# A new issue order for a fused attention and gated feed-forward kernel on one core

## The chip, the core and the metric

The kernel runs on one core of a Trainium2 chip. Five engines with queues of their own work on it: TensorE (PE in the profile; PEld is its loading of weights), VectorE (DVE), ScalarE (ACT), GpSimd (POOL) and SyncE (SP), which here does nothing but issue all DMAs. Each engine works through its instructions in the order in which they were issued, and waits where an operand or a buffer is not there yet. The metric is device time in microseconds, the median of several runs.

## What is computed

```python
scores = scale * np.matmul(x, state.transpose(0, 1, 3, 2))      # B, H, S, D = 8, 8, 512, 64; 32 states
a = softmax(scores);   xread = np.matmul(a, state)
scores2 = scale * np.matmul(state, x.transpose(0, 1, 3, 2))
a2 = softmax(scores2); sread = np.matmul(a2, x)
attn = np.concatenate([xread, sread], axis=2)                   # 8 x 544 rows in all, 512 columns
h = attn @ w_in                                                 # 512 -> 1024
solu = h * softmax(h)
ln = (solu - mean) / np.sqrt(var + 1e-06) * g_ln
out = ln @ w_out                                                # 1024 -> 512
```

Everything is float32 in and out. (`softmax` stands for the reference's lines with maximum, exp and sum.)

## The kernel before

The rows of `attn` are cut into 34 tiles of 128 rows: tiles 0 to 31 are token reads, four for each of the eight batches b, and tiles 32 and 33 are the state reads. The attention's second product is folded into the weights: since `xread @ w_in` is `a @ (state @ w_in)`, the kernel forms state times w_in for each b once and multiplies the softmax with it.

Most products of fp32 data are made as three products of fp32r parts (high times high, high times low, low times high). An operand is split by a copy (the high part) and a difference (the low part). Batch 0's h products, tiles 0 and 1's output products, and everything on the small states are plain fp32 instead, and each such product has two entries in the profile.

The work is cut into named steps, written as Python generators; each name below is a token of the order. A token runs the step to its next `yield`.

- `l0`..`l7` load half row blocks of w_in (`l0 l2 l4 l6` are the left halves), `l8`..`l15` load w_out, `Ls` the states, `LT` and `Ln` the two layouts of x, `Lg` the gains. Each load but the gains is half a megabyte. `cl` and `c` turn a loaded weight (64-bit words) into fp32: one ScalarE step, two VectorE steps and an addition on VectorE or GpSimd.
- `G` copies the states on GpSimd. `V b n` multiplies the states of batch b with half n of w_in (eight small fp32 products, tiles swps or swph in PSUM) and copies the result out. For b of 2 and above it goes to DRAM and back (`Y`, `Z`) until `P` splits it (tiles swh, swl). For b of 0 and 1 it stays.
- `S b` makes the scores of a batch (eight small products), `A b` (`Ah` for batch 0) the softmax of the token reads (tile a, then ath and atl), `E b` that of the state reads with a bounce through DRAM (e2d, e2), and `R b` their reads (srps, srT, sreadT).
- `H t` makes h of tile t (ps_h, two PSUM tiles), `C t` the chain on it (maximum, exp, product, shift by the mean, square, four tiny GpSimd steps for the scale), `D t` transposes u in blocks and sends it through DRAM and back (ut, back), `T t` splits the transposed u (uh, ul), and `O t` multiplies with w_out, scales and stores (o, osb).
- `wi` splits w_in, which only the state reads' tiles need whole; `wg` scales w_out by the gains and `wo` splits it.
- `K` is a warm-up: a product of the identity with itself on TensorE, whose result nobody reads.

What sets the order around everything is the string ORDER: `issue` walks it and runs one step of the named generator at each token, with no scheduler behind it. Since each engine takes its instructions in that order, ORDER is five queues in one. The table OPT names, step by step, the engine of every copy, difference and similar operation (`a`, `d`, `p` for ScalarE, VectorE, GpSimd). Tiles of 4 KB a row come from one pool of 45 slots, so a load also waits for the last reader of its slot; PSUM has two tiles for h and four single banks.

## Time and profile before

| | |
|---|---|
| median of 3 runs | 379.31 us (378.69 to 380.57) |
| span of the profiled execution | 375.6 us; what lies around it is not in the profile, the median is 3.7 us above the span |
| TensorE clock granted, mean | 0.990 |
| DMA | 92.17 MB, mean 245 GB/s |
| idle of GpSimd's scale steps, waiting for ScalarE's square | 57.3 us |
| idle of ScalarE's exp, waiting for the maximum on VectorE | 40.8 us |

How to read the lines that follow below: the page's first line has each engine's busy time, share and instructions; its digit rows cut the span in 40 slices and give busy tenths. A row of the view of stretches has, for a start and an end, busy time and count by engine, the granted clock, the share of DMA time and GB/s. A row of the chain has start, duration, engine, tensor, line and count. A row of the timeline has start, duration, engine, line, operation, output and input with their shapes, the count, and in brackets how long the engine was idle before and what ended that. A row of the grouped view ends with total busy us, mean ns of one, and the idle time before.

### The profile page before, as it was taken

Reading aid. Unit: us, or ns where it says so; the run is one execution under the profiler, and the core shown is the slowest. Engines: PE = TensorE matmul, PEld = TensorE weight load, DVE = VectorE, ACT = ScalarE, POOL = GpSimd, SP = SyncE. Lnnn points to the kernel's source line nnn. Section 1 sums busy time; section 2 is a strip of 40 time slices with the busy share of each in tenths; the row PEclk is TensorE's granted clock in tenths of the full one; section 3 lists DMA queues with packets and bytes.
Section 4 is the critical chain, followed back from the end, with each engine's and each line's share of the span. In section 5 each row is a group of like instructions: output and inputs, shape, how many; then the busy total and the mean of one; then the engine's idle time right before and its main releaser. Section 6 shows DMA issues by size and latency. Waiting matters only on the chain.

```text
span 375.6 us, 6452 instructions
## 1 busy us (share of the span) xinstructions
PE 360.5 (96%) x2382; PEld 266.7 (71%) x2382; DVE 316.7 (84%) x436; ACT 202.5 (54%) x332; POOL 156.3 (42%) x220
## 2 busy tenths in 40 slices
...
PEclk9999999889999999999999999999999999999999
...
GB/s 250 408 393 389 209 314 415 407 292 246 184 264 193 283 298 273 259 306 278 270 316 182 271 272 383 199 119 126 298 169 173 203 134 225 61 294 94 140 168 58
DMA packets 47050, 92.17 MB, mean 245 GB/s; under 512 B 4140, under 2 KB 25900, under 8 KB 47020
## 3 DMA queue, kind: packets, MB, share of 16 engines
...
## 4 chain that ended last, share of the span: by engine, by line
PE 65%; DVE 17%; issue 6%; DMA 6%; ACT 3%; POOL 1%; SPq 0%; DVEq 0%; POOLq 0%
PE o L535 32%; PE h L461 20%; PE warm L559 6%; DMA back<-ut 5%; DVE u L474 3%; PE swps L188 2%; DVE ub L498 2%; DVE ul L136 2%; PE sps L188 2%; DVE sm L468 1%; DMA ut<-ub 1%; DVE a L383 1%; PE swph L188 1%; DVE z L378 1%; PE srps L410 1%
## 5 line engine op out<-in xcount | busy, mean ns | idle before, releaser
L535 PE MATMUL o<-wohi,ul 128*128 128x512 f32 (+1 forms) x264 | 71.5, 385 | 1.0 <-DVE ul L136 1.0
L535 PE MATMUL o<-wohi,uh 128*128 128x512 f32 (+1 forms) x264 | 70.9, 385 | 1.0 <-ACT uh L131 0.8
L535 PE MATMUL o<-wolo,uh 128*128 128x512 f32 (+1 forms) x264 | 70.9, 384 | 0.0
L136 POOL TENSOR_TENSOR ul<-back,uh 128x512 fp32r<-128x512 f32 x33 | 45.4, 1382 | 55.8 <-ACT uh L131 30.7
L471 ACT ACTIVATE e<-h,sm 128x1024 f32<-128x1024 f32 x34 | 37.8, 1113 | 40.8 <-DVE sm L468 40.8
L535 PEld LDWEIGHTS o<-wohi,uh 128*128 128x128 f32 x264 | 48.4, 188 | 12.4 <-ACT uh L131 1.2
L535 PEld LDWEIGHTS o<-wohi,ul 128*128 128x128 f32 x264 | 48.4, 188 | 11.1 <-DVE ul L136 1.4
L468 DVE TENSOR_REDUCE sm<-h 128x1 f32<-128x1024 f32 x34 | 41.3, 1214 | 17.1 <-ACT osb L542 12.4
L535 PEld LDWEIGHTS o<-wolo,uh 128*128 128x128 f32 x264 | 48.5, 188 | 9.8
L486 ACT ACTIVATE e<-u 128x1024 f32<-128x1024 f32 x34 | 36.0, 1058 | 31.9 <-DVE u L481 31.5
L474 DVE SCALAR_TENSOR_TENSOR u<-h,e 128x1024 f32<-128x1024 f32 x34 | 41.1, 1212 | 3.9 <-ACT e L471 3.9
L498 DVE STREAM_TRANSPOSE ub<-u 128x1024 f32<-128x1024 f32 x34 | 41.9, 1236 | 1.8 <-ACT u L479 1.2
L461 PE MATMUL h<-swh,ath 128*128 128x512 f32 x112 | 36.4, 409 | 2.8 <-DVE u L474 2.7
L542 ACT ACTIVATE osb<-o,sm 128x512 f32<-128x512 f32 (+1 forms) x25 | 16.6, 664 | 37.2 <-PE o L535 32.9
L461 PE MATMUL h<-swl,ath 128*128 128x512 f32 x112 | 35.9, 406 | 0.0
L461 PE MATMUL h<-swh,atl 128*128 128x512 f32 x112 | 35.4, 397 | 0.0
L490 POOL TENSOR_TENSOR sm<-sm 128x1 f32<-128x1 f32 x34 | 9.7, 285 | 57.8 <-ACT e L486 57.3
L461 PEld LDWEIGHTS h<-swh,ath 128*128 128x128 f32 x112 | 21.2, 194 | 10.5 <-issue 5.9
L131 ACT ACTIVATE uh<-back 128x512 fp32r<-128x512 f32 (+1 forms) x38 | 23.4, 623 | 8.3 <-DMA back<-ut 8.2
L479 ACT ACTIVATE u<-u,sm 128x1024 f32<-128x1024 f32 x17 | 19.5, 1149 | 13.5 <-DVE u L474 13.3
L559 PEld LDWEIGHTS warm<-ident 128*128 128x128 f32 x182 | 23.3, 211 | 4.8 <-issue 3.4
L461 PEld LDWEIGHTS h<-swl,ath 128*128 128x128 f32 x112 | 20.9, 193 | 7.2 <-issue 1.7
...
## 6 DMA issues: line engine op xcount, KB each, us to landing
ut<-ub SPq DMA_DIRECT2D x34, 512.0 KB, 3.5
back<-ut SPq DMA_DIRECT2D x34, 512.0 KB, 4.4
...
xT<-xT_dram SPq DMA_DIRECT2D x16, 512.0 KB, 7.2
xn<-xn_dram SPq DMA_DIRECT2D x16, 512.0 KB, 7.3
kept<-vt SPq DMA_DIRECT2D x12, 512.0 KB, 7.7
swf<-kept SPq DMA_DIRECT2D x12, 512.0 KB, 6.8
raw<-w_in_dram SPq DMA_DIRECT2D x8, 512.0 KB, 8.2
```

The lines of the kernel that those rows point to most:

```text
L131: nc.scalar.activation(out, src, AF.Copy)
L136: engine(k).tensor_tensor(out=out, in0=a, in1=hi.bitcast(F32), op=ALU.subtract)
L188: nc.tensor.matmul(banks[j][at:at + NS, :], state_of(b, head), moving(head // 2)[h * D:(h + 1) * D], start=True, stop=True)
L461: nc.tensor.matmul(ph[t][:, cols], left[l][:, p, tok], right[r][:, cols], start=(p, l, r) == (0, 0, 0), stop=(p, l, r) == (parts - 1, *kin ...
L468: nc.vector.tensor_reduce(nm, ph[t], AX.X, ALU.max, negate=True)
L471: nc.scalar.activation(e, ph[t], AF.Exp, bias=nm, accum_out=z)
L474: nc.vector.scalar_tensor_tensor(out=u, in0=ph[t], scalar=1.0, in1=e, op0=ALU.mult, op1=ALU.mult, accum_out=su)
L479: nc.scalar.activation(u, u, AF.Identity, bias=su, scale=-float(DF))
L486: nc.scalar.activation(e, u, AF.Square, scale=float(DF) ** -0.5, accum_out=ss)
L498: nc.vector.transpose(ub, us[t][0])
L535: nc.tensor.matmul(po, ut[t][l][:, f, :], w[NP + f // 2][:, f % 2, cols], start=(hf, l, w is wohi, q) == (0, 0, True, 0), stop=(hf, l, q) ...
L559: nc.tensor.matmul(warm, ident, ident, start=True, stop=True)
```

## The change

No step is rewritten. ORDER is a new string, and OPT names other engines for some operations. By the number of instructions: VectorE gives to GpSimd seven swl differences, eight weight conversions, three ul, two atl, a wlo and a wolo difference and four of the softmax's subtractions and products; VectorE gives four ath, two swh and nine uh copies to ScalarE and takes from it four copies out of V's banks, two w_in and one w_out split copies, two scalings and six shifts of u.

```diff
-OPT = dict(ph=2, k4=45, direct=[0, 1], hn=[0], vh=[0, 1], ah=[0], on=[0, 1], s2='pppp', add='dpdpdpdpddpddddp',
-           whi='aaaa', wlo='dddp', wg='aaaaaaaa', woh='aaaa', wol='dpdp', ev='aaaaaaaaaaaaaaaaaaaaaaaaaaaaaaaa',
-           swh='aaadaadaadaadddad', swl='pppppdpdpdddppdd', sub='dpddpddp', subh='dpdd', mulh='dpdd', mul='pddddpdd',
...
+OPT = dict(ph=2, k4=45, direct=[0, 1], hn=[0], vh=[0, 1], ah=[0], on=[0, 1], s2='pppp', add='ppdpppdppppppppp',
+           whi='dada', wlo='dppd', wg='aaddaaaa', woh='aaad', wol='ppdp', ev='aaaaaaaadaaadaaaadadaaaaaaaaaaaa',
+           swh='aaadaaddaaaaaadd', swl='pppppppppppppppp', sub='dpddppdp', subh='dpdddpdddpdddpdd',
...
 ORDER = """
-K l0 l2 Ls0 l4 Lg l6 l1 l3 c0 cl0 LT00 c0*2 cl2 LT01 c2*3 G0 Ls2 c4 cl4 l5 G0 c4 l7 cl6 l8 c4 c6 cl1 Lg c6*2 c1 cl3
-Ln00 K*60 V00 c3*2 V10 c1 Ln01 V00 c3 V00 V20 V10 Ln10 V10 c1 V20 l9 V20 K*5 V30 G2 wi0 c5 l10 G2 c5 V30 l11 V30
...
+l0 l4 c0*2 c4 cl0 c0 K l2 c4 c2 K*3 c2 l6 c6 K*5 cl4 c4 Ls0 cl2 l3 l5 c2 cl6 G0 c6*2 c5*2 G0 V30*2 LT00 LT01 c3*2 V00
+V30 V20*2 cl5 c5 K*2 cl3 K l7 cl7 l1 V00 c7 l9 Ls2 c7 S0 Ah00 c1 c3 Ah00 c1 K Ah00*2 c7 l8 Lg*3 K cl1 c1 V10 V20 E0 Lg
...
```

Three places show what the order does. The first is SyncE's queue at the start of the program, before (raw is a loaded weight block, st the states, gT the gains, xT a layout of x):

```order
L209 DMA raw_85<-w_in_dram 128x1024
L209 DMA raw_87<-w_in_dram 128x1024
L165 DMA st_89<-stB_dram 128x1024
L209 DMA raw_91<-w_in_dram 128x1024
L156 DMA gT<-g_dram 128x2x1
L209 DMA raw_94<-w_in_dram 128x1024
L209 DMA raw_96<-w_in_dram 128x1024
L209 DMA raw_98<-w_in_dram 128x1024
```

and the same queue after:

```order
L201 DMA raw_83<-w_in_dram 128x1024
L201 DMA raw_85<-w_in_dram 128x1024
L201 DMA raw_97<-w_in_dram 128x1024
L201 DMA raw_106<-w_in_dram 128x1024
L157 DMA st_118<-stB_dram 128x1024
L201 DMA raw_122<-w_in_dram 128x1024
L201 DMA raw_124<-w_in_dram 128x1024
L185 DMA xT_0_149<-xT_dram 128x1024
```

The four left halves of w_in now come first (before, the fourth was the sixth entry), the states behind them, and the gains move behind the second states' load.

The second place is TensorE's queue at its start, before (warm is the warm-up, swph and swps are V's results, wf the converted w_in, s the states):

```order
L559 MATMUL warm<-ident 128x128 x61
L188 MATMUL swph_0_209<-wf_100,s_0_116 32x512 x2
L188 MATMUL swph_0_209<-wf_112,s_0_116 32x512 x2
L188 MATMUL swph_0_209<-wf_120,s_0_116 32x512 x2
L188 MATMUL swph_0_209<-wf_135,s_0_116 32x512 x2
```

and after (the first V is that of batch 3, then batches 0 and 2, then S0):

```order
L551 MATMUL warm<-ident 128x128 x9
L180 MATMUL swps_0_0_138<-wf_87,s_0_129 32x512 x2
L180 MATMUL swps_0_0_138<-wf_100,s_0_129 32x512 x2
L180 MATMUL swps_1_0_139<-wf_90,s_0_129 32x512 x2
L180 MATMUL swps_1_0_139<-wf_108,s_0_129 32x512 x2
L180 MATMUL swph_0_157<-wf_87,s_0_129 32x512 x2
```

Sixty-one warm-ups became nine ahead of the first V. In the whole program 91 became 23.

The third place is TensorE's queue between the scores of block 1 and those of block 2, before (o is the output of a tile, h_802 and h_811 are tiles 4 and 5; the scores of block 2 follow):

```order
L529 MATMUL o_0_738<-wog_580,uh_729 128x512 x2
L529 MATMUL o_0_738<-wog_742,uh_729 128x512 x2
L529 MATMUL o_0_738<-wog_754,uh_729 128x512 x2
L529 MATMUL o_0_738<-wog_766,uh_729 128x512 x2
L461 MATMUL h_802<-swh_0_778,ath_796 128x512 x2
L461 MATMUL h_811<-swh_0_778,ath_796 128x512 x2
L461 MATMUL h_811<-swl_0_789,ath_796 128x512 x2
L461 MATMUL h_802<-swl_0_789,ath_796 128x512 x2
L461 MATMUL h_811<-swh_0_778,atl_805 128x512 x2
L461 MATMUL h_811<-swh_1_787,ath_796 128x512 x2
L461 MATMUL h_802<-swh_0_778,atl_805 128x512 x2
L461 MATMUL h_802<-swh_1_787,ath_796 128x512 x2
```

and after (o_0_655 is tile 0, o_0_672 tile 1, h_743 tile 4):

```order
L521 MATMUL o_0_655<-wog_617,uh_637 128x512 x2
L521 MATMUL o_0_672<-wog_554,uh_657 128x512
L521 MATMUL o_0_672<-wog_617,uh_657 128x512 x2
L521 MATMUL o_0_655<-wog_609,uh_637 128x512 x2
L521 MATMUL o_0_672<-wog_609,uh_657 128x512
L521 MATMUL o_0_655<-wog_698,uh_637 128x512 x2
L453 MATMUL h_743<-swh_0_420,ath_712 128x512 x2
L453 MATMUL h_743<-swl_0_572,ath_712 128x512 x2
L521 MATMUL o_0_672<-wog_609,uh_657 128x512
L180 MATMUL sps_0_756<-xT_0_695,s_0_129 32x512 x4
L180 MATMUL sps_1_757<-xT_1_619,s_0_129 32x512 x4
```

Before S2 there now stand 14 output products of tiles 0 and 1 in place of 8 of tile 0, and 4 h products in place of 16.

More of the change, by code (lines that the diff above doesn't have):

```diff
@@ L27 @@
 NTILES = B * NT + B * NS // P
-OPT = dict(ph=2, k4=45, direct=[0, 1], hn=[0], vh=[0, 1], ah=[0], on=[0, 1], s2='pppp', add='dpdpdpdpddpddddp',
-           whi='aaaa', wlo='dddp', wg='aaaaaaaa', woh='aaaa', wol='dpdp', ev='aaaaaaaaaaaaaaaaaaaaaaaaaaaaaaaa',
-           swh='aaadaadadaadddad', swl='pppppdpdpdddppdd', sub='dpddpddp', subh='dpdd', mulh='dpdd', mul='pddddpdd',
-           ath='aaddaddd', alo='dddpddpd', up='aaadaadaaaddddaaaaadddddaaddaddadd',
-           uh='aadaaaaaaaadaaddaaaaadaadaaadddddadddaaddddaaddadaaaaaaddddaddaadadd',
-           ul='ppppdpdpppdppdpddpdppddpddpddddppdddpdpddppppdppdddddpppppdpppddppdp',
-           oe='aaaaaaaddaaaaaaaaaadadddadaaaddada')
@@ L83 @@
-T30 H32*2 O28 T30 O28 T30 O28*3 O29 O28 O29*2 T31 C32 O28 O29*2 T31 O29 C32 O29*2 T31 C32 O29*3 T31 O29 C32 O30*2
-D32 C32 O31 O30 O29 O30 D32 C32 O30 C33 O29 O30*3 C33 O30 O31 D32 O30 C33 O30*2 C33 O31*2 D33 C33 O31*2 O30 O31 D33
-C33 O31 O30 T32 O31*2 T32 O31 O32 O31 T32 D33 O32 O31 T32 O32*2 O31 O32*6 T33 O32 T33 O32 T33 O33 O32 O33 T33 O33*3
-O32 O33*23
+OPT = dict(ph=2, k4=45, direct=[0, 1], hn=[0], vh=[0, 1], ah=[0], on=[0, 1], s2='pppp', add='ppdpppdppppppppp',
+           whi='dada', wlo='dppd', wg='aaddaaaa', woh='aaad', wol='ppdp', ev='aaaaaaaadaaadaaaadadaaaaaaaaaaaa',
+           swh='aaadaaddaaaaaadd', swl='pppppppppppppppp', sub='dpddppdp', subh='dpdddpdddpdddpdd',
+           mulh='ppdddpdddpdddpdd', mul='pdpdppdd', ath='aaaadaaa', alo='dppdddpp',
+           up='adddddadddddddddaaaaadddddaddaaadd',
+           uh='aaaddaadaaaaaaaadaaadaaadaaaddaaaaaaaaaaaaadddaddddaaadaddaaadadadaa',
+           ul='ppppppdpdpppppppdppdppdpdddddpdddpdddpdpppdppdppddpppddppdppppdddpdp',
+           oe='aadaaaaaadaaadaadddaadaaddaaaaddaa')
@@ new lines @@
+ORDER = """
+l0 l4 c0*2 c4 cl0 c0 K l2 c4 c2 K*3 c2 l6 c6 K*5 cl4 c4 Ls0 cl2 l3 l5 c2 cl6 G0 c6*2 c5*2 G0 V30*2 LT00 LT01 c3*2 V00
+V30 V20*2 cl5 c5 K*2 cl3 K l7 cl7 l1 V00 c7 l9 Ls2 c7 S0 Ah00 c1 c3 Ah00 c1 K Ah00*2 c7 l8 Lg*3 K cl1 c1 V10 V20 E0 Lg
+V10*2 Ah01 K*2 G2 Ah00 l10 Ah00 V00 K*2 E0 K*2 E0 K*3 Ln00 E0 G2 V11 Ah00 V11 E0*2 Ah01*2 V40 Ah00*2 V40 V11 V01 V40
+V01 V50 H0 V01 Lg l12 c8 c9 c8 c12 l11 Ah01 V50*2 cl8 l13 Ah01 l14 V21*2 H0 V21 cl10 c10 E0 c12 cl12 c12 P11 Ah01 l15
+V60*2 H1 c11 H1 C0*2 V60 Ah01 LT10 LT30 E0*2 P10 C0*2 LT11 V31 C0 V31 Ah01*2 H2 P11 C1 D0 V70 c9 V31 C1 Ln01 H2 c8 V70
```

78 lines of the change are left out of this document (35 added, 43 removed).

## Prediction

> **What bounds the kernel now.** I read the page's busy shares first, then its clock line, then a few stretches of time, then the chain that ended last.
>
> ```profile
> PE 360.5 (96%) x2382; PEld 266.7 (71%) x2382; DVE 316.7 (84%) x436; ACT 202.5 (54%) x332; POOL 156.3 (42%) x220
> PEclk9999999889999999999999999999999999999999
> ```
>
> ```profile
> core 0: us, PE busy (x) PEld busy (x) DVE busy (x) ACT busy (x) POOL busy (x), PEclk, DMA share, GB/s
> 70.00:80.00 10.00, 7.71 (x26) 4.83 (x34) 9.96 (x11) 7.66 (x13) 7.90 (x10) 0.66 0.96 372
> 80.00:290.00 210.00, 208.87 (x1350) 161.15 (x1335) 199.97 (x269) 114.79 (x188) 100.63 (x139) 1.00 0.71 243
> 290.00:310.00 20.00, 17.77 (x135) 13.52 (x133) 18.36 (x25) 9.54 (x15) 3.65 (x7) 1.00 0.52 178
> ```
>
> ```profile
> 1.34 16.39 PE warm L559 x122
> ...
> 20.47 1.31 PE warm L559 x10
> 21.78 1.02 PE swps L188 x16
> ...
> 24.11 1.02 PE sps L188 x16
> ...
> 32.63 1.91 PE h L461 x4
> ...
> 237.41 13.15 PE o L535 x58
> ...
> 324.43 0.94 PE h L461 x4
> ...
> 370.62 0.47 ACT osb L542
> ```
>
> TensorE is busy 96% of the span, and from 80 to 290 us it idles 1.1 us while VectorE is busy 200 of 210: two engines are full at once. The chain shows the pitch of TensorE's work: 227 ns for an fp32r product of 512 columns (13.15 / 58), 1.02 us for a group of eight small fp32 products (V or S), 131 ns for a warm-up entry. The profile has two entries for each fp32 product; the 182 warm-up entries are 91 products in the code, and 182 x 131 ns = 24 us of the 360 are no work. The change leaves 46 entries, 6 us; every other product stays. So 18 us of "busy" goes, but the span shortens only by what the next wait allows. I therefore count by stages with three marks: the first H product (32.6), the scores of block 1 (S1, 57.6) and of block 2 (S2, 79.7), and the last product (370.6).
>
> **Stage A, up to the first H: 4.0 us earlier.**
>
> ```profile
> 4.72 0.68 ACT L221 ACTIVATE r<-raw 128x512 uint32<-128x512 uint32 x1 [2.73 <-DMA raw<-w_in_dram]
> 5.98 0.68 ACT L221 ACTIVATE r<-raw 128x512 uint32<-128x512 uint32 x1 [0.57 <-DMA raw<-w_in_dram]
> 8.10 1.65 POOL L133 COPY s<-st 64x512 f32<-64x512 f32 x2 [6.81 <-DMA st<-stB_dram]
> 12.89 0.69 DVE L238 CUSTOM_DVE_ANT_0 wf<-wf,r 128x1024 uint16<-128x1024 uint16 x1
> 17.66 1.95 PE L188 MATMUL swph<-wf,s 64*32 64x512 f32 x32
> ```
>
> Before, the operands of the first V were complete at 12.89 + 0.69 = 13.6 us (the last conversion of a first-half w_in tile), but the 122 warm-up entries stood ahead of it in TensorE's order until 17.7: they cost 4 us. After, the loads stand as l0 l4 l2 l6, then the state. A half-megabyte load lands 1.26 us after the one before it (4.72, 5.98), the state took 2.1 (5.98 to 8.10), so w_in is there at 4.72 + 3 x 1.26 = 8.5 and the state at 10.6. Its two copies on GpSimd take 1.65: the first V starts at 12.2 (conversion ends before, near 11). Nothing but 18 warm-up entries runs ahead, until about 4 us, so TensorE stands idle for 8.
>
> ```profile
> 57.62 1.09 PE L188 MATMUL sps<-xT,s 64*32 64x512 f32 x16
> 61.05 6.28 PE L529 MATMUL o<-wog,uh 128*128 128x512 f32 x14 [0.42 <-ACT uh L131]
> 70.07 1.12 PE L529 MATMUL o<-wog,uh 128*128 128x512 f32 x2 [2.74 <-ACT wog L256]
> 73.41 2.33 PE L461 MATMUL h<-swh,ath 128*128 128x512 f32 x4 [2.22 <-DVE u L474]
> 79.67 1.09 PE L188 MATMUL sps<-xT,s 64*32 64x512 f32 x16
> ```
>
> What that idleness costs is seen at 70 to 80: after waits of 2.74 and 2.22 us the granted clock was 0.66 over ten microseconds, which is 0.5 for 6.8 of them, and four fp32r products took 2.33 instead of 0.94 us. A V at half clock costs one more microsecond. Between 0 and 5 us (five groups) I take 2.5. The Trainium skill, "TensorE: Matmul & The Clock Gate" (Part 1: The HAM clock gate), says that the half rate is the resting state and that about 3.4 us of sustained work lifts it. By that my estimate of the cost would be half of 3.4, 1.7 us, and the sum 0.8 lower; the 6.8 us of the trace, with work in only part of them, neither bear this out nor exclude it. S0 then starts at 12.2 + 3.1 + 2.5 + 0.8 (six warm-up entries) = 18.6 instead of 24.1. From S0 to the first H took 8.5 us before (24.11 to 32.63), a chain of VectorE and ScalarE steps on the scores that is still there. I add 1.5, as H0's PSUM tile is now freed by ScalarE's copies of V11, which queue behind the softmax: first H at 28.6.
>
> **Stage B, to S1: one microsecond lost again.** It took 25.0 us before. The order has 22 us of TensorE work here, where it had 24.5 with warm-ups, but VectorE has as much as before (26 us by its rows). New is that R0 stands ahead of S1 and waits for a bounce through DRAM while the loads that were pulled forward are still landing.
>
> ```profile
> back<-ut SPq DMA_DIRECT2D x34, 512.0 KB, 4.4
> 52.00 8.34 DMA back<-ut
> ```
>
> Such a transfer lands after 4.4 us as a rule, and after 8.3 in the crowded stretch. Two of them (out and back) cost between 0 and 8 more; most of it lies beside V and H products, I take 1. S1 at 54.6.
>
> **Stage C, S1 to S2: 3.7 us gained.** Before it took 22.1 us, with TensorE idle for 0.42 + 2.74 + 2.22, and the half clock on top. The waits ended with ScalarE's scaling of w_out and with block 1's softmax. After, the w_in splits (three casts, three differences) are out of the stage, so that the scaled w_out comes sooner, and O0 and O1 (14 products) fill the wait for the softmax, where O0 alone (8) did before. That softmax chain is unchanged: 14.7 us from the end of S1 (58.7) to H4 at 73.41. S2 stands 1.9 us of products after that: 1.1 + 14.7 + 1.9 = 17.7, and I put 0.7 on it for GpSimd's fuller queue. S2 at 54.6 + 18.4 = 73.0 instead of 79.7. If that cover is too thin and the clock falls again, 3.4 us come back.
>
> **Stage D, S2 to the last product: 0.9 us gained.** It took 290.9 us. Six more O products (0.9 each, by 6.28 / 7) and twelve fewer H products (0.227) are done before S2: -2.7. Next, the engines.
>
> ```profile
> L136 DVE TENSOR_TENSOR swl<-swf,swh 128x1024 fp32r<-128x1024 f32 x7 | 9.6, 1375 | 0.0
> L136 POOL TENSOR_TENSOR swl<-swf,swh 128x1024 fp32r<-128x1024 f32 x7 | 17.2, 2455 | 0.8 <-DVE swh L133 0.7
> L238 DVE CUSTOM_DVE_ANT_0 wf<-wf,r 128x1024 uint16<-128x1024 uint16 x10 | 6.8, 684 | 0.6
> L238 POOL TENSOR_TENSOR wf<-wf,r 128x512 uint32<-128x512 uint32 x6 | 8.5, 1424 | 16.2 <-DVE wf L235 9.3 <-ACT r L221 6.9
> L481 DVE TENSOR_SCALAR u<-u,sm 128x1024 f32<-128x1024 f32 x17 | 16.5, 978 | 0.3
> ```
>
> Seven swl differences leave VectorE (-9.6 us) for GpSimd (+17.2), eight conversions (-5.5, +11.4), six shifts of u come to VectorE (+5.9); all changed rows by the means of this grouped view give VectorE -24, GpSimd +51, ScalarE -3. VectorE is then at 293 of about 368, 80% against 84, GpSimd at 207. I summed VectorE's rows from S2 to each tile's transpose, and TensorE's to that tile's first O product: the distance fell to 6.3 us at tile 22 before, less than the way through DRAM, and the trace shows the stalls that follow.
>
> ```profile
> 291.79 0.73 PE L535 MATMUL o<-wohi,ul 128*128 128x512 f32 x2 [0.96 <-DVE ul L136]
> 293.02 0.70 PE L461 MATMUL h<-swh,ath 128*128 128x512 f32 x2 [0.50 <-DVE u L474]
> ```
>
> After it never falls under 12.5. So the idle time of the stretch from 290 to 310 goes (20 - 17.77): -2.2. What is late next is the chain of one tile. From its last H product to its first O product there lie 27 us of other products on average before, 22 after, with 16.8, 15.6 and 15.4 at tiles 4, 25 and 33.
>
> ```profile
> 269.99 1.23 DVE L468 TENSOR_REDUCE sm<-h 128x1 f32<-128x1024 f32 x1 [0.41 <-PE h L461]
> ...
> 287.31 0.43 DVE L133 CAST uh<-back 128x512 fp32r<-128x512 f32 x1 [2.17 <-DMA back<-ut]
> ```
>
> ```profile
> 343.83 1.23 DVE L468 TENSOR_REDUCE sm<-h 128x1 f32<-128x1024 f32 x1 [6.00 <-ACT osb L542]
> ...
> 356.63 0.63 ACT L131 ACTIVATE uh<-back 128x512 fp32r<-128x512 f32 x1
> ```
>
> The first view is that chain on a full VectorE: 269.99 to 287.74, 17.8 us; the second near the end: 13.4. At 17.8 the three short tiles lack 5.6 together, at 13.4 nothing. I take +4. The end is unchanged: 5.0 us from the last product, and tile 33's chain (13.4) just fits in its 15.4.
>
> ```profile
> 265.31 1.91 POOL L373 TENSOR_TENSOR a<-a,m 128x1024 f32<-128x1024 f32 x1
> 266.64 1.14 DVE L133 CAST swh<-swf 128x1024 fp32r<-128x1024 f32 x1
> ...
> 279.32 0.69 DVE L133 CAST ath<-aT 128x1024 fp32r<-128x1024 f32 x1
> ```
>
> GpSimd's extra work is not free for VectorE: a cast of 1024 columns took 1.14 us beside a GpSimd subtraction and 0.69 after it. With GpSimd busy 15 points more of the time (207 of 368 for 156 of 376), some 110 casts, shifts and differences lose 0.15 x 0.45 each, 7 us of the 24 freed: inside the slack. The Trainium skill, "SBUF — State Buffer" (Who interferes with whom), speaks against moving work there: the two engines take turns at one pair of ports, and the second waits until the first has finished its whole instruction. By that a row would wait for half a 2.4 us difference on average, an estimated 20 us in all; VectorE would be near 313 again, the 2.2 us of stalls would stay, and the sum would be 373.9.
>
> **Sum.** -4.0 + 1.0 - 3.7 - (2.7 + 2.2 - 4.0) = -7.6: a span of 368.0 for 375.6. The median of the runs, 379.3, is 3.7 above the profiled span; with that, 371.7 us.
>
> **Rivals.** *Chains too short (slower), 0.18.* If the chain of a tile takes 20.6 us because SP and GpSimd hold it up (GpSimd's 2.4 us differences now stand between the small steps that scale a tile), the lacks add to 28 us by the order, against 11 before. Half of it paid, as a wait at one tile lengthens the next one's lead, is +14 in place of +4: 382, up to 390. It decides from about 19.5 us on. For it: SP's bounces queue behind waits for buffers. Against: VectorE, which made the 17.8, is emptier. *Early gain given back, 0.12.* TensorE stays at half clock between the short pieces up to S1, and R0 waits the full 8 us: A gives 2.5, B loses 4, C gives 1.5, D 0.9: 378.4. That would also be the picture if the warm-ups had been covering a wait and nothing else. *The waits hidden (faster), 0.15.* If short leads cost nothing and the first products run at full clock, -4.0 and -2.5 more: 365, down to 362.
>
> **Chances.** The forecast, 366 to 376, has 0.55. About 0.5% is what a measurement of this kernel can tell from no change, 377.4 to 381.2. Faster: 0.55 + 0.15 + a little of the second rival = 0.71; within: 0.11; slower: 0.18. The range 363 to 382 leaves out the ends of the first and third, and takes in the bounds of the unknown costs: the half clock (0 to 5), R0's bounce (0 to 8) and the short leads up to 14.
>
> **What would show it.** Right: first V near 12 us with a clock below 1, first H before 30, S2 near 73, no VectorE wait on TensorE's rows past 290, VectorE near 293 us busy. Wrong: S2 later than 78 (stages A to C), a clock of 0.5 at any time after 30 us, or waits of O products for uh, ul or back spread over the middle (short chains); then TensorE's busy share past 80 us falls under 97%.

## The result and the profile after

The changed kernel is slower: 390.27 us (387.88 to 392.65) against 379.13 for the kernel before in the same comparison, a ratio of 1.031 (1.025 to 1.037). The forecast was 371.7 us, with a range of 363 to 382. The profiled execution took 388.81 us, with a span of 387.0.

The marks of the prediction, each from the first or last row of its products in the timeline of TensorE:

| mark (us from the start of the span) | before | forecast | after |
|---|---|---|---|
| first H product | 32.6 | 28.6 | 30.2 |
| scores of block 1 (S1) | 57.6 | 54.6 | 53.6 |
| scores of block 2 (S2) | 79.7 | 73.0 | 75.7 |
| S2 to the last product (stage D) | 290.9 | 290.0 | 303.7 |
| last product to the end | 5.0 | 5.0 | 7.6 |

Stages A to C came 4 us early, 2.7 less than forecast. Stage D lost all of it and 8.8 us more, although 2.7 us of its products had already been done. The page of the kernel after, its busy shares and the granted clock by slices:

```profile
PE 350.6 (91%) x2246; PEld 253.3 (65%) x2246; DVE 312.1 (81%) x411; ACT 199.7 (52%) x331; POOL 197.4 (51%) x246
PEclk9699998999999999999889999999999999999997
```

VectorE has 25 instructions fewer than before, but is busy 312.1 us, where the forecast had 293. The rows of the change are gone from it, and those that are left take longer: counted by the means of the grouped views, the rows that moved are worth about 22 us, and the rows that stayed take about 16 us more than before (6 of them in the weight conversions of the first 62 us). Stretches of time of the kernel after (columns: the stretch, its length, then busy time and count of TensorE, its weight loads, VectorE, ScalarE and GpSimd, the granted clock, the DMA share, GB/s):

```profile
80.00:290.00 210.00, 199.44 (x1227) 154.87 (x1227) 188.25 (x243) 112.67 (x186) 118.14 (x147) 0.98 0.74 261
290.00:310.00 20.00, 17.68 (x134) 13.44 (x134) 17.63 (x19) 6.07 (x9) 9.35 (x12) 1.00 0.46 159
80.00:360.00 280.00, 265.13 (x1640) 207.26 (x1640) 235.99 (x301) 143.76 (x236) 146.92 (x190) 0.99 0.66 231
```

Between 80 and 290 us TensorE idled 1.1 us before and now 10.6. The stall at 290 to 310 that was to go is still there (17.68 of 20 busy, before 17.77). The last row covers 80 to 360 us, a stretch that lies inside stage D in nearly every run below: TensorE idles 14.9 of 280 us. I use it as the measure of stage D; before it was this:

```profile
80.00:360.00 280.00, 276.64 (x1708) 215.59 (x1693) 248.86 (x333) 143.31 (x235) 125.01 (x179) 1.00 0.66 225
```

That is 3.4 us of idle time. Where such idle time arises is seen in the chain that ended last, at the worst place of the kernel after (columns: start, duration, engine, tensor, line, count):

```profile
168.60 1.26 DVE ub L490
169.87 7.45 DMA ut<-ub
...
177.38 4.26 DMA back<-ut
...
182.38 2.94 DVE ul L128 x2
185.32 1.14 DVE sm L460
186.46 1.16 DVE aT L378
...
187.64 0.70 DVE ath L125
...
188.37 3.27 DVE atl L128
```

A tile's way through DRAM is late (7.45 us for its first transfer, where the median of such transfers is 3.3), VectorE waits for it in line, then runs two ul differences, and the softmax of the next batch stands behind them. The same place in the timelines of GpSimd and TensorE (in brackets the idle time before a row and what ended it; dots stand for rows left out), and the granted clock of the next ten microseconds in a row of the view of stretches:

```profile
181.81 2.36 POOL L128 TENSOR_TENSOR swl<-swf,swh 128x1024 fp32r<-128x1024 f32 x1
...
187.69 2.87 POOL L128 TENSOR_TENSOR wlo<-wf,whi 128x1024 fp32r<-128x1024 f32 x1 [3.51 <-DVE aT L378]
```

```profile
183.50 0.74 PE L527 MATMUL o<-wohi,uh 128*128 128x512 f32 x2 [1.36 <-ACT osb L534]
...
188.48 0.70 PE L453 MATMUL h<-swh,ath 128*128 128x512 f32 x2 [1.02 <-DVE ath L125]
189.02 0.62 PE L453 MATMUL h<-swl,ath 128*128 128x512 f32 x2
191.70 1.22 PE L453 MATMUL h<-swh,atl 128*128 128x512 f32 x2 [2.05 <-DVE atl L128]
192.72 1.05 PE L453 MATMUL h<-swh,ath 128*128 128x512 f32 x2
```

```profile
190.00:200.00 10.00, 8.30 (x25) 6.68 (x26) 9.28 (x11) 4.34 (x7) 5.01 (x11) 0.66 0.27 100
```

Two ul took 2.94 us while GpSimd ran a swl difference, and an atl took 3.27 while GpSimd ran a wlo difference. In the kernel before they take 2 x 0.68 and 1.24 us on average (rows further below). TensorE waits 1.02 and 2.05 us for what comes of it, and then its products take 1.05 us a pair instead of 0.62: the granted clock from 190 to 200 us was 0.66. So there were four suspects: the **lead** of the tiles (products between a tile's last H and its first O product), the **buffers** that late outputs hold, the **start** (no warm-ups, work put off), and **GpSimd's wide rows** beside VectorE's.

### The profile page after: what moved, and what is told of

The parts are those of the page before. It is cut to its first block, busy times and chain, and to the rows that moved or that the text cites. A ratio compares the mean times of both kernels' runs of the same rounds, so it can differ in the third digit from the quotient of the medians.

```text
span 387.0 us, 6187 instructions
## 1 busy us (share of the span) xinstructions
PE 350.6 (91%) x2246; PEld 253.3 (65%) x2246; DVE 312.1 (81%) x411; ACT 199.7 (52%) x331; POOL 197.4 (51%) x246
## 4 chain that ended last, share of the span: by engine, by line
PE 36%; DVE 32%; DMA 13%; issue 7%; ACT 5%; POOL 4%; SPq 1%; DVEq 0%; ACTq 0%; POOLq 0%
PE o L527 20%; PE h L453 12%; DMA back<-ut 5%; DVE u L466 5%; DMA ut<-ub 5%; DVE sm L460 4%; DVE ub L490 3%; DVE ul L128 3%; PE swps L180 2%; DVE u L473 2%; DMA st<-stB_dram 2%; DMA out_dram<-osb 2%; DVE uh L125 2%; ACT e L478 1%; DVE sc L330 1%
## 5 line engine op out<-in xcount | busy, mean ns | idle before, releaser
L128 POOL TENSOR_TENSOR ul<-back,uh 128x512 fp32r<-128x512 f32 x36 | 48.6, 1357 | 76.3 <-ACT uh L123 56.8
L527 PE MATMUL o<-wohi,uh 128*128 128x512 f32 (+1 forms) x264 | 73.4, 389 | 9.0 <-ACT osb L534 3.4
L527 PE MATMUL o<-wohi,ul 128*128 128x512 f32 (+1 forms) x264 | 72.6, 390 | 0.8 <-DVE ul L128 0.7
L527 PE MATMUL o<-wolo,uh 128*128 128x512 f32 (+1 forms) x264 | 73.0, 384 | 0.0
L527 PEld LDWEIGHTS o<-wohi,ul 128*128 128x128 f32 x264 | 48.6, 190 | 12.2 <-DVE ul L128 2.0
L466 DVE SCALAR_TENSOR_TENSOR u<-h,e 128x1024 f32<-128x1024 f32 x34 | 41.3, 1215 | 14.8 <-ACT e L463 14.7
L128 POOL TENSOR_TENSOR swl<-swf,swh 128x1024 fp32r<-128x1024 f32 x14 | 35.0, 2501 | 17.8 <-issue 11.2
L123 ACT ACTIVATE uh<-back 128x512 fp32r<-128x512 f32 (+1 forms) x47 | 28.5, 621 | 23.8 <-DMA back<-ut 23.6
L453 PE MATMUL h<-swh,ath 128*128 128x512 f32 x112 | 35.6, 401 | 1.3 <-DVE ath L125 1.0
L453 PE MATMUL h<-swl,ath 128*128 128x512 f32 x112 | 35.6, 399 | 0.9 <-POOL swl L128 0.9
L128 DVE TENSOR_TENSOR ul<-back,uh 128x512 fp32r<-128x512 f32 x28 | 24.3, 874 | 12.5 <-ACT uh L123 12.3
L230 POOL TENSOR_TENSOR wf<-wf,r 128x512 uint32<-128x512 uint32 x14 | 18.3, 1311 | 25.5 <-DVE wf L227 13.8
L534 ACT ACTIVATE osb<-o,sm 128x512 f32<-128x512 f32 (+1 forms) x24 | 15.8, 663 | 28.9 <-DMA out_dram<-osb 8.7
L453 PEld LDWEIGHTS h<-swh,atl 128*128 128x128 f32 x112 | 21.3, 192 | 7.8 <-DVE atl L128 2.5
```

Of the source, the lines that this page charges most:

```text
L123: nc.scalar.activation(out, src, AF.Copy)
L128: engine(k).tensor_tensor(out=out, in0=a, in1=hi.bitcast(F32), op=ALU.subtract)
L230: engine(of("add", n)).tensor_tensor(out=w, in0=w, in1=rounding[n], op=ALU.add)
L453: nc.tensor.matmul(ph[t][:, cols], left[l][:, p, tok], right[r][:, cols], start=(p, l, r) == (0, 0, 0), stop=(p, l, r) == (parts - 1, *kin ...
L466: nc.vector.scalar_tensor_tensor(out=u, in0=ph[t], scalar=1.0, in1=e, op0=ALU.mult, op1=ALU.mult, accum_out=su)
L527: nc.tensor.matmul(po, ut[t][l][:, f, :], w[NP + f // 2][:, f % 2, cols], start=(hf, l, w is wohi, q) == (0, 0, True, 0), stop=(hf, l, q) ...
```

## The experiments

Sixteen kernels ran. The table has for each the median, the ratio to the kernel before on the same chip with its interval, the length of stage D (S2 to the last product), TensorE's idle time from 80 to 360 us, and VectorE's and GpSimd's busy time over the span. The last four columns are of the one profiled execution.

| kernel | us | ratio | stage D | idle | VectorE | GpSimd |
|---|---|---|---|---|---|---|
| before | 379.1 | 1 | 290.9 | 3.4 | 316.7 | 156.3 |
| after | 390.3 | 1.031 (1.025 to 1.037) | 303.7 | 14.9 | 312.1 | 197.4 |
| new order, old engines | 420.0 | 1.107 (1.100 to 1.115) | 332.1 | 31.4 | 322.8 | 148.7 |
| old order, new engines | 390.2 | 1.031 (1.023 to 1.039) | 301.2 | 8.1 | 309.3 | 200.2 |
| new start, old rest | 385.8 | 1.019 (1.011 to 1.027) | 300.7 | 11.2 | 319.3 | 172.8 |
| old start, new rest | 391.2 | 1.033 (1.027 to 1.039) | 301.8 | 13.3 | 310.5 | 176.5 |
| after, four output buffers | 390.7 | 1.030 (1.024 to 1.037) | 305.2 | 14.6 | 311.0 | 197.5 |
| after, six sum buffers | 391.6 | 1.036 (1.030 to 1.041) | 303.1 | 13.7 | 318.7 | 197.1 |
| after, leads longer | 408.1 | 1.077 (1.069 to 1.084) | 316.8 | 22.0 | 314.0 | 197.3 |
| before, leads shorter | 416.2 | 1.099 (1.092 to 1.105) | 327.6 | 21.7 | 318.5 | 156.0 |
| after, chain without the bounce | 388.5 | 1.029 (1.025 to 1.032) | 302.6 | 13.2 | 315.9 | 197.8 |
| after, no swl | 378.7 | 1.002 (1.000 to 1.005) | 291.9 | 6.6 | 302.1 | 161.8 |
| after, small operations for swl | 380.4 | 1.003 (0.999 to 1.007) | 294.6 | 6.9 | 301.6 | 197.6 |
| after, swl by the old table | 393.8 | 1.040 (1.034 to 1.045) | 312.4 | 18.3 | 321.3 | 183.1 |
| before, all swl on GpSimd | 383.3 | 1.013 (1.008 to 1.018) | 295.5 | 7.1 | 314.8 | 171.6 |
| before, 52 fewer warm-ups | 371.7 | 0.984 (0.979 to 0.989) | 288.4 | 1.3 | 317.2 | 158.5 |
| before, 82 fewer warm-ups | 373.7 | 0.989 (0.985 to 0.994) | 290.8 | 3.0 | 317.0 | 158.7 |
| new start, old rest, spread | 377.7 | 0.998 (0.994 to 1.002) | 299.1 | 9.7 | 318.5 | 169.6 |

### The two halves of the change, each alone

The order and the engine table were crossed. First the changed kernel with the whole old OPT:

```diff
...
-           swh='aaadaaddaaaaaadd', swl='pppppppppppppppp', sub='dpddppdp', subh='dpdddpdddpdddpdd',
+           swh='aaadaadaadaadddad', swl='pppppdpdpdddppdd', sub='dpddpddp', subh='dpdd', mulh='dpdd', mul='pddddpdd',
...
```

> The new order with the old engine choices. Three theories of the 13.7 us that stage D (scores of block 2 to the last product) takes longer than forecast. Order: the chains of the tiles have too few products to cover them, and SP, VectorE and ScalarE stand in order behind waits; then the order alone carries the loss, 386 to 392 us, with TensorE idle again 12 us or more past 80 us. Engines: GpSimd holds 197 us instead of 156 and slows VectorE's rows; then the order with the old choices gains what stages A to C gained, 374 to 378 us. Late outputs: as Order, since the place of the output transfers in SP's queue is part of the order.

Then the kernel before with the whole new OPT:

```diff
...
-           swh='aaadaadaadaadddad', swl='pppppdpdpdddppdd', sub='dpddpddp', subh='dpdd', mulh='dpdd', mul='pddddpdd',
+           swh='aaadaaddaaaaaadd', swl='pppppppppppppppp', sub='dpddppdp', subh='dpdddpdddpdddpdd',
...
```

> The old order with the new engine choices. Order: within 1% of the kernel before, 376 to 383 us, as the old order's chains have 27 us of products on average. Engines: slower by 8 us or more, 387 us up, with the mean of the 512-column differences on VectorE at 0.87 us where the kernel before had 0.68. Either way GpSimd is near 200 us busy, so the mean of those rows tells whether the load of GpSimd or the order makes VectorE's rows long.

The order alone costs 41 us, the engines alone 11, both together 11. So they are not two parts whose prices add up: the new table takes 30 us off the new order. The first result is past the range of every theory and remains unexplained; the second fell where the engine theory put it, and its VectorE rows are longer by what the theory named, if less (ul 0.80 us on average, for 0.68).

### Where in time: starts and rests

The new order up to S2 was joined to the old one for all that was left, and the other way round. Each step ran once, and took the engine of the part in which it ran.

```diff
 H4*2 D3*2 E1 O1 E1*2 S2
-D3 A2 T2 E1 H4 O0 H4 Z20 H4*2 Y60 H5 C4*2 E1 C4 H5*3 Ln20
+Ln10 wi0 wi1 wi2 Ln20 Y40 Y41 wi1 Y60 wi0 Z20 C1 Y61 Y70 wi2 Z21 H5*3 O0 H5 H4*2 LT31 LT40 C2
...
```

> The new order and engines up to the scores of block 2, then the old order and engines for all that is left (the warm-up products that stood later in the old order are left out, as in the new one). If the whole loss is in stage D, by whatever cause, and the early gain of 4 us is real: 374 to 377 us. If what was pulled forward or put off in the new start (no warm-ups, clock at half rate, splits of w_in late) is paid for later: 379 us or more.

```diff
 H5 O0 H5 C3 D2 H4 E1 H4 S2
-...
+wo4 T1 Z31 O1*2 T1 O1 wo5 wo4 D2 wo6*2 O1*2 wo5 wo7 D3*2 E1 O1 E1*2 D3 A2 T2 E1 H4*2 C4*2
...
```

> The old order and engines up to the scores of block 2, with all 182 warm-up entries, then the new order and engines for all that is left: the counterpart of the new start with the old rest. Loss in stage D as such: the scores of block 2 come at 79.7 us as in the kernel before, the rest takes 14 to 20 us longer than its 291, 393 to 400 us. If the loss in D came from what the new start leaves behind (transfers and splits put off): 379 to 386 us.

The new rest behind the old start has a stage D of 301.8 us, so the loss is in the new rest as such, as expected for that theory (the total is 2 us under its bound, since S2 came 1 us earlier and the loss was 11). But the new start with the old rest was no gain either: 385.8, a miss. Its loss lies behind the seam. The chain of that run:

```profile
83.96 7.81 DMA kept<-vt
91.77 11.17 DMA e2d<-e2b
103.00 3.98 DMA e<-e2d
```

The join issues eleven half-megabyte transfers within 11 us, nine of which the new start had put off (the two of x's layout, LT31 and LT40, stand there in the old order too), with the splits of w_in, and the softmax of the state reads stands behind them. So it was tried again with those spread out:

```diff
-S2 Ln10 wi0 wi1 wi2 Ln20 Y40 Y41 wi1 Y60 wi0 Z20 C1 Y61 Y70 wi2 Z21 H5*3 O0 H5 H4*2 LT31 LT40 C2
+S2 Z20 C1 H5*3 O0 H5 H4*2 LT31 C2 Ln10 H5 C3 H5 H4*2 C3 C4*2 wo7 A2 C4 Z21 O1*2 wi3 E1 D3 C4 H6
...
```

> The new order and engines up to the scores of block 2 and the old rest, as in the run that came to 385.8 us, but with the eleven transfers and the splits of w_in that the new start puts off spread over the next 40 us and more, not issued at once. If the 7.4 us that TensorE idled behind that run's seam (80 to 120 us) came from that burst: 366 to 374 us, faster than the kernel before. If the new start as such is paid for later: 379 us or more.

The spread gives 8 us back (385.8 to 377.7), so issuing transfers and splits in one burst did cost about that. It is still no gain on the kernel before, and it fell between the two expectations (366 to 374 us, or 379 and more). TensorE was idle 4.4 us at 80 to 120 us, and S2 came at 75.1, so the early gain was there and was lost behind S2. What the new start leaves undone by then was not taken apart further.

### Buffers

```diff
-    SLOTS = dict(k4=OPT["k4"], o=2, s2=2, m1=1, z1=1, r=1, sc=2, sm=4, rr=3)
+    SLOTS = dict(k4=OPT["k4"], o=4, s2=2, m1=1, z1=1, r=1, sc=2, sm=4, rr=3)
```

> The changed kernel with four instead of two buffers for the scaled output rows (osb), nothing else. Late outputs: the new order puts some output transfers 20 to 30 us of products behind their tile's last product, so the scaling two tiles later waits for the buffer and holds its PSUM bank; with four buffers the waits of osb for out_dram (12.7 us in sum) go, the end after the last product falls from 7.6 to 5 us, and the time to 380 to 385 us. Order: only the end gets shorter, 387 to 389 us, and TensorE's waits for uh, ul, ath and u in the middle stay.

```diff
-    SLOTS = dict(k4=OPT["k4"], o=2, s2=2, m1=1, z1=1, r=1, sc=2, sm=4, rr=3)
+    SLOTS = dict(k4=OPT["k4"], o=2, s2=2, m1=1, z1=1, r=1, sc=2, sm=6, rr=3)
```

> The changed kernel with six instead of four slots for the small buffer of a tile's sums, nothing else. VectorE's maxima wait 11 us for the scaling of four tiles back, which frees that buffer. Buffer theory: those waits stretch the chains, and without them the time falls to 381 to 386 us. Short leads: the leads are as before the edit, so the time stays within 1%, 386 to 392 us; this run is also the base for the run with longer leads.

In the kernel after, the waits on output buffers are these (columns: engine, line, what for, total us, times, longest; the two engines' last ones stand ahead of the last two outputs):

```profile
ACT osb L534 <- DMA out_dram<-osb: 8.7, 3, 6.1
DVE osb L536 <- DMA out_dram<-osb: 4.0, 1, 4.0
```

With four buffers they are gone and the way from the last product to the end falls from 7.6 to 5.9 us, but stage D is as long as before the edit and the time is the same. With six slots for the sums VectorE's 11 us of waits for them are gone, and the time is the same again. Neither buffer sets the pace.

### Leads and the length of a chain

This was the first theory. Followed row by row over tiles 4 to 33, a chain takes 21.7 us from its maximum to the end of the first half of ul (20.8 before), and not the 17.8 and 13.4 of the two views that the prediction used; the mean lead is 22.1 us. So short leads looked like the whole answer. The O products were moved later in the new order, and earlier in the old one, one example of each:

```diff
-H21 T17 C19 P50 H21 C16 O17*2 A6 O17*2 C19 H20*2 A5 H20 C19 O17 R4 D19 H20*3 A6 O16 O17*2 Z60
+H21 T17 C19 P50 H21 C16 A6 O16 C19 O16 H20 O16 H20 A5 O16 H20 C19 O16 R4 D19 O17 H20 O17 H20*2 A6 O17 Z60
...
-    SLOTS = dict(k4=OPT["k4"], o=2, s2=2, m1=1, z1=1, r=1, sc=2, sm=4, rr=3)
+    SLOTS = dict(k4=OPT["k4"], o=2, s2=2, m1=1, z1=1, r=1, sc=2, sm=6, rr=3)
```

> The changed kernel with the O products (and the scaling and output transfer behind them) of tiles 4 and up moved later by up to 5 us of TensorE's products, growing over the first 60 us of stage D; all else keeps its order. More tiles are then open at once, so the small buffer of a tile's sums (sm) has six slots instead of four. The mean lead (products between a tile's last H and its first O product) goes from 22.1 to 25.6 us, and the sum by which leads fall short of 21.7 us, the mean length of a chain measured from the maximum to the first half of ul, from 40 to 12 us. Short leads: the waits of O products for uh and ul in the middle nearly go, TensorE's idle time past 80 us falls from 15.5 to about 6, and the time to 377 to 384 us. If VectorE's longer rows and waits set the pace (contention, engines): unchanged, 386 to 392 us.

```diff
-H19 A6 C18 D17 H20 T16 H20 H19 C18 P51 H19 D18 H19 O15 C18 H19*2 Ln51 A5 O15 O16 D18 O16 Ln60 C19
+H19 A6 C18 D17 O16 H20 T16 O16 H20 O16 H19 C18 P51 H19 D18 H19 C18 H19*2 Ln51 A5 D18 O16 Ln60 C19
...
```

> The old kernel (old order, old engines) with the O products of tiles 4 and up moved earlier by up to 5 us of TensorE's products, where their operands allow it; all else keeps its order. The mean lead falls from 27.0 to 23.9 us, and the sum by which leads fall short of 21.7 us rises from 19 to 38, as in the changed kernel (40). Short leads: TensorE stalls on uh and ul in stage D, and the time rises to 383 to 392 us. If the lead is not what counts: 377 to 381 us, as the kernel before.

Longer leads made the new kernel 16.5 us slower than its base with six slots, the opposite of what the theory said and past the other range too; shorter ones made the old kernel 38 us slower, far past both. A shift of one kind of product is no clean test: it also moves that product against the H products that stand in the same queue. In both runs VectorE's maxima then waited for H products (view of the waits from 75 us on: engine, line, what for, total us, times, longest):

```profile
DVE sm L456 <- PE h L449: 18.1, 8, 6.0
```

```profile
DVE sm L459 <- PE h L452: 19.2, 7, 7.7
```

The first row is of the new order with longer leads, the second of the old one with shorter leads; the kernels after and before have 3.6 and 3.4 us there. So the chain was to be cut instead, with the order left alone:

```diff
         back[t] = block([DF], F32, f"back{t}")
-        from_dram(back[t], d)
+        from_dram(block([DF], F32, f"back{t}"), d)
+        back[t] = ub
```

> The changed kernel, in which uh and ul are made from ub itself and not from its copy that went through DRAM; both transfers are still issued at their place, but nothing reads what they bring, so the output is not the reference's. A tile's chain, 21.7 us on average from its maximum to the first half of ul, loses the 10.7 us from the end of ub to the start of uh; engines, their rows, the traffic and the order stay. Short leads: the products no longer wait for uh and ul, TensorE's idle time past 80 us falls under 6 us, and the time to 372 to 380 us. VectorE's longer rows beside GpSimd set the pace: within 1% of the changed kernel, 386 to 392 us.

388.5 us, 1.8 less than the kernel after, which the intervals of the two ratios don't tell apart. The grouped rows of this run (columns: line, engine, operation, output and inputs, count, then busy us, mean ns of one, idle time before):

```profile
L121 DVE TENSOR_TENSOR ul<-ub,uh 128x512 fp32r<-128x512 f32 x28 | 28.0, 1007 | 0.7 <-ACT uh L116 0.5
L116 ACT ACTIVATE uh<-ub 128x512 fp32r<-128x512 f32 x44 | 26.6, 619 | 0.1
```

The waits for the way through DRAM are gone: ScalarE's uh waited 23.6 us in sum for it in the kernel after, and VectorE's ul 12.3 us for ScalarE; now it is 0.1 and 0.5. Yet uh starts 10.0 us after ub on average, where it was 10.7: the two engines come to these rows no earlier, as the rows ahead of them in their queues fill the time, and VectorE's rows got longer (ul 1.01 us for 0.87, 315.9 us busy for 312.1). So the run did not shorten the chains as meant (21.2 us for 21.7). It shows that taking away the waits for the bounce gains almost nothing here. That the mean length of the chain does not decide the time either is seen by setting it beside a run below that has almost the same, 21.1 us, and takes 380.4.

### GpSimd's wide rows

```diff
-        lo = block([DF], F32R, f"swl{b}_{j}")
-        minus(of("swl", 2 * b + j), lo, swf[b, j], hi)
-        sw[b, j].append(lo)
+        sw[b, j].append(hi)
```

> The changed kernel without the low part of the state products (swl): its products read the high part instead, so the output is not the reference's, and 14 of GpSimd's 2.5 us differences (35 us) are gone; VectorE's rows and the order stay. Contention with GpSimd: VectorE's differences of 512 columns go from 0.87 us back towards 0.68, VectorE is busy 303 us or less instead of 312, and the time falls to 378 to 385 us. Short leads: VectorE's rows may shrink, but the chains keep the bounce and the waits in line; 386 to 391 us.

378.7 us: 11.6 us went, and stage D is 291.9 us long, where 290.0 was forecast. VectorE runs the same rows as in the kernel after and is busy 10 us less. But three other things went with the rows: GpSimd's queue is shorter, TensorE no longer waits for swl (0.9 us in the kernel after), and the pool of 45 slots has 14 tiles fewer to hold (SyncE's loads waited 9.2 us in sum for a reader of a slot in the kernel after, 4.8 us here). The next run separates the first; the last run of this section keeps the other two as they were.

```diff
-        minus(of("swl", 2 * b + j), lo, swf[b, j], hi)
-        sw[b, j].append(lo)
+        for _ in range(4):
+            nc.gpsimd.tensor_tensor(out=scratch, in0=scratch, in1=mhalf, op=ALU.pow)
+        sw[b, j].append(hi)
```

> The changed kernel, in which each of the 14 swl differences on GpSimd is replaced by four small operations of GpSimd (one column, a power, 0.6 us each by the rows of sm, 2.4 us together) and the products read the high part instead, so the output is not the reference's. GpSimd is as long busy as in the changed kernel (within 3 us of 197), in the same places, but without the wide reads and writes. Port theory (wide rows of GpSimd stretch VectorE's rows beside them): like the run without swl, VectorE near 302 us busy and 376 to 382 us. Queue theory (what stands behind swl in GpSimd's queue comes late, whatever swl does): like the changed kernel, 386 to 391 us.

GpSimd is busy 197.6 us in the same places (after: 197.4), and the time is 380.4 us. Grouped rows (columns: line, engine, operation, output and inputs, count, then busy us, mean ns, idle time), first of this run, then of the kernel after, then of the kernel before:

```profile
L294 POOL TENSOR_TENSOR scratch<-scratch,mhalf 128x1 f32<-128x1 f32 x56 | 35.6, 636 | 3.4
L121 DVE TENSOR_TENSOR ul<-back,uh 128x512 fp32r<-128x512 f32 x28 | 20.5, 737 | 10.1 <-ACT uh L116 10.0
L121 DVE TENSOR_TENSOR atl<-aT,ath 128x1024 fp32r<-128x1024 f32 x3 | 3.7, 1229 | 0.0
```

```profile
L128 DVE TENSOR_TENSOR ul<-back,uh 128x512 fp32r<-128x512 f32 x28 | 24.3, 874 | 12.5 <-ACT uh L123 12.3
L125 DVE CAST uh<-back 128x512 fp32r<-128x512 f32 x20 | 12.3, 621 | 0.1
L128 DVE TENSOR_TENSOR atl<-aT,ath 128x1024 fp32r<-128x1024 f32 x3 | 6.7, 2244 | 0.0
L490 DVE STREAM_TRANSPOSE ub<-u 128x1024 f32<-128x1024 f32 x34 | 42.1, 1238 | 5.6 <-ACT u L471 4.7
L128 POOL TENSOR_TENSOR swl<-swf,swh 128x1024 fp32r<-128x1024 f32 x14 | 35.0, 2501 | 17.8 <-issue 11.2 <-DVE swh L125 5.4 <-DVE uh L125 0.9
```

```profile
L136 DVE TENSOR_TENSOR ul<-back,uh 128x512 fp32r<-128x512 f32 x31 | 21.1, 680 | 1.0 <-ACT uh L131 0.5
L133 DVE CAST uh<-back 128x512 fp32r<-128x512 f32 x29 | 12.1, 423 | 7.9 <-DMA back<-ut 7.9
L136 DVE TENSOR_TENSOR atl<-aT,ath 128x1024 fp32r<-128x1024 f32 x5 | 6.2, 1238 | 0.0
L498 DVE STREAM_TRANSPOSE ub<-u 128x1024 f32<-128x1024 f32 x34 | 41.9, 1236 | 1.8 <-ACT u L479 1.2
```

The small operations fill GpSimd for the same 35.6 us, and VectorE's atl is back at 1.23 us from 2.24, its ul at 0.74 from 0.87. So of the 11.6 us, 9.8 are won with a GpSimd that is as busy but not wide; some 1.8 are left for its queue, which the spread of either run doesn't resolve. The wait for swl and its pool slots are gone in this run too, so the 9.8 us still hold their share. The rows also show which operations are stretched: ul, atl (two operands in SBUF) and uh (a copy), but not ub (1.238 for 1.236).

Could the seven differences that the change took from VectorE simply go back?

```diff
-           swh='aaadaaddaaaaaadd', swl='pppppppppppppppp', sub='dpddppdp', subh='dpdddpdddpdddpdd',
+           swh='aaadaaddaaaaaadd', swl='pppppdpdpdddppdd', sub='dpddppdp', subh='dpdddpdddpdddpdd',
```

> The changed kernel with the old choices for swl alone: 7 of the 14 differences that it computes are on VectorE again, by 1.38 us each instead of 2.5 on GpSimd; order and all other choices stay. Port theory: half of the 12 us that go without swl come back, less what 9.6 us of rows cost on VectorE in places that the order did not mean for them: 383 to 389 us. Queue theory: 380 to 386 us, as GpSimd's queue is shorter. If the order needs its own choices, as the run with all old choices (420 us) suggests: 392 us or more.

No: 393.8 us. VectorE is at 321.3, the 312.1 of the kernel after and 9.6 us of rows, and gets nothing back; the ul rows are even longer (0.96 us). That is outside the ranges of the port and the queue theory and inside the third, that the order needs its own choices; why is open. And the same part of the change, alone, on the kernel before:

```diff
-           swh='aaadaadaadaadddad', swl='pppppdpdpdddppdd', sub='dpddpddp', subh='dpdd', mulh='dpdd', mul='pddddpdd',
+           swh='aaadaadaadaadddad', swl='pppppppppppppppp', sub='dpddpddp', subh='dpdd', mulh='dpdd', mul='pddddpdd',
```

> The kernel before with all swl differences on GpSimd (seven more there, seven fewer on VectorE), nothing else: one part of the change alone. By the means of the rows VectorE loses 9.6 us and GpSimd gains 17.2. Port theory: VectorE gets back part of the 9.6 by longer rows beside GpSimd, and its two-operand rows, 0.68 us in the kernel before, get longer; 380 to 386 us. As I predicted in step D (inside the slack): 377 to 380 us.

383.3 us, 1.3% slower, with swl's tiles and TensorE's need of them unchanged. VectorE lost 9.6 us of rows, but its busy time fell by only 1.9 (316.7 to 314.8): 7.7 us came back as longer rows.

```profile
L128 DVE TENSOR_TENSOR ul<-back,uh 128x512 fp32r<-128x512 f32 x31 | 22.9, 741 | 3.3 <-ACT uh L123 2.8
L128 DVE TENSOR_TENSOR atl<-aT,ath 128x1024 fp32r<-128x1024 f32 x5 | 9.7, 1934 | 0.0
```

In the kernel before, ul takes 0.680 us and atl 1.238: the old order lets hardly any of these rows fall beside a wide row of GpSimd.

### Warm-ups

```diff
-Ln00 K*60 V00 c3*2 V10 c1 Ln01 V00 c3 V00 V20 V10 Ln10 V10 c1 V20 l9 V20 K*5 V30 G2 wi0 c5 l10 G2 c5 V30 l11 V30
+Ln00 K*8 V00 c3*2 V10 c1 Ln01 V00 c3 V00 V20 V10 Ln10 V10 c1 V20 l9 V20 K*5 V30 G2 wi0 c5 l10 G2 c5 V30 l11 V30
...
```

> The old kernel without 52 of the 61 warm-up products that stand ahead of the first V product (104 of 182 entries, 13.6 us of TensorE); nothing else. Stage A as predicted: the first V starts when its operands are there, near 13.6 to 15 us instead of 17.7, and a gain of 2 to 4 us stays to the end, 375 to 377 us. Given back: VectorE or the transfers set the start of the later stages, or TensorE runs at half clock in the first V products, and the time is 378 to 382 us.

371.7 us, 1.6% faster than the kernel before and the fastest of all; the expectation was 375 to 377 us. The timeline of TensorE in this run:

```profile
1.34 4.01 PE L551 MATMUL warm<-ident 128*128 128x128 f32 x18 [1.34 <-POOL ident masks.py:199]
8.55 4.10 PE L180 MATMUL swph<-wf,s 64*32 64x512 f32 x12 [3.20 <-POOL s L125]
13.31 1.48 PE L180 MATMUL swph<-wf,s 64*32 64x512 f32 x18 [0.66 <-DVE wf L230]
...
19.65 1.09 PE L180 MATMUL sps<-xT,s 64*32 64x512 f32 x16
```

The first V runs at 8.55 us as soon as the states are copied, and not near 13.6 us with its last operand, goes on at 13.3 when the next conversion is done, and the first scores come at 19.7 instead of 24.0. These 4.4 us last: S2 is 4.3 us earlier, and stage D is shorter by 2.5, since the stall at 290 to 310 us doesn't arise. The rest of the warm-ups was left out too:

```diff
-V20 K*5 V30 G2 wi0 c5 l10 G2 c5 V30 l11 V30 K*5 S0 c7 cl5
+V20 V30 G2 wi0 c5 l10 G2 c5 V30 l11 V30 S0 c7 cl5
...
```

> The old kernel with nine warm-up products in all (18 entries of 182), the other 30 that the run with 130 entries kept being left out too. Those 30 stand between V, S0 and V of block 0's second half and take 7.9 us of TensorE in order. If they hold back work that is ready: 2 to 5 us faster than that run's 371.7, 367 to 370 us. If they only fill waits for VectorE's softmax and conversions: 371 to 373 us. If the clock falls for want of work: 373 us or more, with a granted clock under 0.8 in the first 30 us.

373.7 us, no faster than with those 30 (the intervals of the ratios overlap). The first H product comes 1.2 us earlier (27.7 for 28.9), but S2 1.2 later. The granted clock was 0.94 over the first 30 us, not under 0.8, the sign that the expectation gave for a falling clock. So those warm-ups hold back nothing that lasts.

## Why the prediction was wrong

**Stages A and B: right as a sum.** The first V was at 11.9 us (12.2), the first H at 30.2 (28.6), S1 at 53.6 (54.6): 1.6 us late and then 1.0 early, so the two errors partly cancel. That removing warm-ups gains about 4 us which stay was confirmed by itself, on the kernel before.

**Stage C: its 3.7 us did not come.** From S1 to S2 it took 22.1 us, as before, where 18.4 was forecast (S2 at 75.7 for 73.0). The O products did fill the wait for the softmax, but TensorE still waited for the scaled w_out ahead of them. Its timeline in the kernel after:

```profile
64.11 9.67 PE L521 MATMUL o<-wog,uh 128*128 128x512 f32 x18 [2.13 <-DVE wog L250]
```

The wait of 2.13 us was for one of the two scalings that the change had moved to VectorE, which was busy 21.9 of these 22.1 us, and the granted clock from 60 to 70 us was 0.83. So the O products ended late, and the H products of tile 4 behind them began 18.6 us after the end of S1, where the prediction counted 14.7.

**Stage D: the step that failed** is the one that priced GpSimd's extra work at "7 us of the 24 freed: inside the slack". VectorE ended 19 us above the forecast (312.1 for 293), about 16 of them by longer rows, and they were not in the slack. The price had been read from one copy beside a subtraction (1.14 for 0.69 us) and spread evenly over 110 rows. But two-operand rows are hit harder (3.27 us for 1.24 in the place above), and a wide row of GpSimd that falls on VectorE just ahead of what TensorE waits for costs at full price, and then the clock. The prediction had set beside it the Trainium skill, "SBUF — State Buffer" (Who interferes with whom), and worked out VectorE near 313 by it: the trace agrees with that figure, at 312.1. That it fits to 1 us is in part luck, since the wait of half a row was assumed and 6 of the 16 us fell in the weight conversions. The sum that I drew from it, 373.9, still fell short, as it let the longer rows cost 2.2 us only. The section also says that reductions never meet this, that two operands in SBUF do, and that copies can: here the maxima (1.214 before, 1.215 us after, by the means of their groups) and the differences and copies above bear that out.

**The term "+4" for short leads** had a chain that was too short (17.8 us from one tile; the mean over 30 tiles is 21.7), and by that reading the rival *Chains too short*, with 382 to 390, named almost the measured time. It had the time, but its mechanism isn't borne out: chains of 21.2 and 21.1 us went with 388.5 and 380.4 us, and without the waits for the bounce only 1.8 us went. Leads could not be changed alone, so that part is not excluded; as far as the runs show, its fit was luck.

**The end**, "unchanged", was 2.6 us longer. The new order issues several output transfers 20 to 30 us of products behind their tile, so the last outputs wait for a buffer; with four buffers 1.7 of the 2.6 went, though not from the total.

**The signs that the prediction named** for stage D came as it said they would if it was wrong: a clock of 0.66 at 190 us, waits of O products for uh and ul spread from 126 to 315 us, and TensorE's busy share past 80 us under 97% (265.1 of 280). S2 later than 78 us, its sign for stages A to C, did not come.

How far the cause reaches: without GpSimd's wide swl rows stage D is 291.9 to 294.6 us of the 303.7, so 9 to 12 of the 13.7 us above the forecast went with them. These are all fourteen wide swl rows, and seven of them ran on GpSimd before; moving the other seven, alone and in the old order, cost 4.8 us, and moving them back in the new order gained nothing. So that wide rows of GpSimd stretch VectorE's and cost time is shown, and how much of the loss each moved row bears is not. What stays open is why the new order needs its own table (420 us with the old one), what its shorter leads add, and why the new start's lead is lost behind S2 even where the old rest follows it.
